# Row thresholds moved from VectorE to ScalarE, products with V of two units in one burst, and a new order of the whole program

## Chip, cores and metric

One NeuronCore of a Trainium2 chip runs the program. The metric is the device time of one execution in microseconds (us). TensorE, VectorE, ScalarE, GpSimd and SyncE appear in rows as PE, DVE, ACT, POOL and SP; PEld is TensorE's weight load.

## What is computed

Attention over 4 batches, 8 heads, 576 tokens and a head size of 64, then two feed-forward parts on 2304 tokens of 512 numbers:

```python
scores = scale * np.matmul(q, k.transpose(0, 1, 3, 2))
thresh = np.max(scores, axis=-1, keepdims=True) - tau
scores = np.where(scores >= thresh, scores, -1000000000.0)
attn = np.exp(scores - np.max(scores, axis=-1, keepdims=True))
attn = attn / (np.sum(attn, axis=-1, keepdims=True) + 1e-09)
x = np.matmul(attn, v)             # -> 2304 x 512
h = x @ w_in;  x = (h - np.tanh(h)) @ w_out
...                                # 8 experts: each token goes through the one with the largest logit
out[mask] = gate_w[mask, None] * eom[mask, e, None] * (np.maximum(x[mask] @ w1[e], 0.0) @ w2[e])
```

Of each row only the scores within `tau` of the row's maximum count.

## The kernel before

**Attention.** There are 32 units: a batch, a half of its tokens (256 or 320 queries) and a pair of heads, in this order, so a batch has four units of the first half and then four of the second. `attention(ui, ...)` (L1051) records one unit. For each tile of 128 queries and each head TensorE makes the scores `sp` in PSUM (L1085, in the first eight units L1096). VectorE scales them into `em` and keeps each row's minimum of the negated scores in `mx` (L1106, called **scan** below). ScalarE makes the exponentials `e` (L1109). The **threshold** is one addition for the tile: `tb = mx + tau`, 2 numbers per partition for both heads, or 1 for a third tile that both heads share (L1118, with the choice of engine in L1113). The **gate** (L1122, VectorE) keeps the exponentials whose score passes `tb` and sums each row into `rs`. TensorE turns the gated tile (`pt`, L1138), ScalarE moves it to SBUF (`eth`; the rest `elh`), and TensorE multiplies it by V (`pv`, L1193): ten matmuls per unit that write 64 columns of the array, issued as a burst of six and one of four (`BURST = (3, 2)`), between which other work may stand. The reciprocal sums are spread by ScalarE (`rb`, L1171), turned (L1208), and VectorE multiplies the result by them (`xf`, L1212).

**Feed-forward.** As soon as units have filled a chunk of 256 tokens, steps of the first feed-forward part on that chunk (`step`, L731: matmuls L743 and L777, ScalarE L756 to L762, VectorE L764 and L766, GpSimd L556) stand between the attention's instructions. VectorE also unpacks this part's weights (`conv`, L685 to L694). After the attention come the rest of this part, the routing and the eight experts.

**What sets the order.** Every instruction is recorded with an engine, a duration for the planner and the tiles that it reads and writes. `Sched.order` then plays the program through and writes each engine's instructions in the order of their start, by a table of numbers (`URGENCY`), one for each instruction. So one number moves rows on every engine, and an instruction whose planner duration changes can move too. Each engine then works through its list in order. Tiles come from rings: `em` has 5 buffers, `e` 3, `eth` and `elh` 2, `rb` 3 (`EMN, EN, ETN, RBN`).

`round_to` and `rest` (L551 to L575) are helpers, so their lines L554, L556, L558, L568 and L574 stand for many operations.

Of the kernel before, what the change touches and what calls it, by code (L numbers as in the profile page):

```python
# [17 lines left out]
ALU = mybir.AluOpType  # L18
# [34 lines left out]
EMN, EN, ETN, RBN = 5, 3, 2, 3  # L53
# [28 lines left out]
    'c-rk)_e0I^`+n_p_Bm}WqbRdfA{k{gsFV_gG^vo35s{EmR%GN|WF{+ARyJj&ge0<8Ml!NWzW4L$^Iv>De#m*9bDrlO*L_{rb24W{Y~J<E^zPq+'  # L82
    '8H0`2J<ACSua*BeJtTN*M&IV|;fvEYmpGpG+ZFq6U4%dD7VBweWWrVdSa2~~mzrN`=UzQII^M2R1@Y-vX*fNp$#=(@@Mz}2y{huJ9Q|~uO>c9%'
    '+hxvAjz>4G^j=Ch&F);+ZMk9bTccMaVssXDy}#@IwLJ<y{nC)w;;JI)I1_xLPM6@C#doi4J>zFEYv<kdm1Z%WUfeWpmSheH(chdEW%)L&xWG5L'
    'aBpidJ=hKp?5s`;vY7w-N8ql9GqsBk4VYP^iCJ*<q21U%^Hy{Y-sC*wlB?dgMTx$KEi0}rk5rUnQ++mmKC>g%XJ@V%u@Ad^ys)#@%hSY?5aN-w'
    'jeb?e?ebgB>b<=riQWDVi5jqaoaq*qSy`d8H@q3@UezsJ?`n#txm874QOTQ~kE&MvB+K|ihEIFZ-v>V!QR<r~_kLUU?PS&CXKY!6{p?Z83H>2g'
    'k{g$q&j~s8ZnFC7@$z!((}^pO+YO)9G{LtZB;mo8HBYb1xKbN<xZf&y{$t0`;x<1s8|-#jxsThH<)4^ZrFQ1{O+%Y&`UeL%>37K1RCqk^IIo9E'
    't$){hkC*3|o=8+MIWmvr$%-|1J688Muz2d>KHVnxSc0la?*#q9Y&G8Me=_n|Xv(&=Khl&FhXfuNGoa-*6Gd!OccunMyKPF}-0%7eZ~K--p$D`r'
    '^Uep<$sYM$IOTunkZp6!@w6WN*B!Q(p3m0G5kl(y3YHGv;PiN5*zCT+JL>`h2iIM#KAVy^dETIP)w1PP>w^vqsb8(Hs`^=+f5Fu8?(YRQWo6p8'
    '7w-7oafa2>ng12M%CG2TX07_F7&zVB>g8S4%NTXRCc`P6PE4Ek^H={9(@VaXnyzT*dM)9)bI$TbQ;Q1&_f*vSzbYf=pQt}PARuAJ0ea#~yY2HW'  # L90
    '>bFNEoHH-o>bJ6M>dWIUznW@3F3`O0Ww}N6GiSh%Wt;XFYHDw#H+FdO+V4ul=BSmf7UA};y<8gl1s?X^RI<56NBT)`>`U4GCSg|Mp~M1>*N!c!'
    'Qhr-#B7QbRGU=Ah!T96}zm<L2micdOHa}hbcjKZt_yzB#_kj^n|7D-{p3$@WSK@1ZxP_C?rDZucmF4@*^?wQ3^^z<n*Xp<<YU8L2t%GA7PsBz|'
    '5?bbr^M4YXPfyZhGX7Bmlhz#es<4Rea<P8$%T33WdJ$TadtHcJdAt)LX&p#k@6h*RpBFltHk^BL^=IYrVe5=PY&p2{o3mA$$?Ec*POtkjSvl*a'
    'W%*kDygaOW*j&HRC#%0huFm9@Ira^id4_SJKQBG1&)UBtu6065v1k0eN<}GlPw&Iw+@KQ&?Gq+mDY5r)oSk{LxB30lZ)W#1KN}rs95B;0bN{Kt'
    '$a^*T6+5djaqDA;Z}qqBJ@(?K84{&y{?@;}cXX)kuerN&a7sl#yMEy=kN1sEH=#C}tJ12r{I1QDUwcs+_hC-ctI=N+WI<vEnefeU&4Iz@9f!sa'
    'H>lZPHTY~!?=f1tH(%-BXTQI9Ug#9eWw1}s>5}w`yL_lFySnQ;ja@I_8>f4D+>~6#YguU};oS7qyy1Gt>|I~yZTX_QfBdgW?7RG`!vzsJlIV@t'
    '6pqiOX20=CTH)|JJyJM#QimP&%J`jk*j3)=m&KBGj`D%V6;q#ES%kh`KY-2r9YUC7evOPSEl*i9`}MStqVM@(nmJPCyf;Rj_S=o0yR?K%j*F`M'
    'IxV|`JH0N&YMIHc;NIEOepGwZM{1g0oiID?Joa*NO2gt$=a=O+U-98)`kWirp)~2>lIq6SF278pJa=d|&)iYj^iXB_@JX53{<-JQ9D3mHvi7Sy'
    'BBGAnFtNPV0;_aiVEAWC(*5uUi!TRb5&Dr1cNa$<zio5u=ir32j5}O)NLs?hOBL5|A7919+#BYwxxuz}%2%(M7s(L6)pLm>_9-W$B<Br!j`Fmw'
    'jIWqFewdYUd{+Zqw+$&z9~aDxjtP0$)NS)n?+LD!U5`$jo~n2^ewanupWLrri_bb@1|xRHt+#P<XnEJ-zw6O<%Yg74Jn4d*I=%5yUH{fFQ;W&c'  # L100
    '2Tp0rCN+3#KRbmbOpBGS`2KZl%bV<?h%>J)xAjkTe(rhOHTO{C+ht?@?=6yOy-d8x`(D3TC%u+&=I!8k?2{qswQARyyE)H;YC7o6IM!o(o_~k)'
    '4T}aWt}{7x*nz4x%o}F$uwQvEj})!ifTPvPOKrZSRSel{QTX@Je-j<98oQ?QM~fc?Et5P>GkFkvrOdHlZ)9cPPpoO-=?D4S)22Pf!j?q0#4g&~'
    'W>oh~-+W=pOQw{+P@jM44gKW^{?n&t<yF6%t{w&MvchPKk})5iA76NSt*v#U=Z9|RzHLp4W@p@SN>~%_YBK9VSpUMG+1fS+KG7ke54QUK{Ai=!'
    'TQYIvj-8~jxr@%2%zEp0BUD)yRw;M1b`PwXw8U=e@Ead%!a4=3C%PtYI9NX?>fWv~xdz@Hbz=OU5BPhhHe=xO8#A%OPKELFEt3}978-{XUF$t)'
    'f`i_@5%2#9UKTSlV#@2rJXSOBiYpEs$ru>&Y*GFaohKQi=7-mHmX{Zwu`-Rkt<`W;+kEOvF6+F3laDd?d3lEa5XJLg%7NRZ<Dd0BvO03b0sfLg'
    'dw-1U^~}SLy|U$pZ)qo$E?D&U!mrrJC7<sM`~8RQaWc!eV!KZF%e|aD{Th00O_(ufR@Sb-E9-xCX)KIn-3}QYCz}@cSyET~rsDXmzJ+_}Po6(U'
    'o=9WsB3-8)dDlVGL+|JDEWIm=iP7FmlyQ?bb(oi-DV)|Kf1a}@{J{R-YR};Bdp0-@j>w35>a(Rt=VLYN+O{{L(koeibGL{|FUF23u>Z=PnmHi%'
    'VEOvf&%5cEb+u7CXBI3T@M={4?9YXnw9$f*+XvnF6CYdq%=&cO<cN|#^IBX6n*KN5eY4g3)`siX{9NpIdd;Zu&G>Bl8n5>6EWP_~cS*-TZ6jn2'
# [347 lines left out]
def tile_main(ctx, tc, qa, qb, q2, kT, k3, vv, tau, w_in, w_out, gates, w1, w1b, w2, out, dbg=None):  # L456
# [594 lines left out]
    def attention(ui, k0, qs):  # L1051
# [132 lines left out]
        xf = buf("ep", "xf", 2, [P, 320])  # L1184
        dl += TAU
        pv = buf("ps_v", "pv", 1, [P, 4, P])
        pvf = lambda: pv.t.rearrange("p a b -> p (a b)")[:, 0:n]

        def pairs_(kts):
            for kt in kts:  # L1190
# [787 lines left out]
```

## Time and profile before

| | |
|---|---|
| time, median of 3 | 970.16 us (969.92 to 971.55) |
| profiled execution | 971.04 us, its span 969.2 us |
| TensorE busy | 940.4 us (97%) |
| VectorE busy | 727.5 us (75%) |
| ScalarE busy | 551.1 us (57%) |
| GpSimd busy | 346.0 us (36%) |
| granted clock of TensorE, mean | 0.998 |

Shares over the whole span mix stages with different limits, so the stretches of the span have to be read apart. A matmul is shown until its end in the pipeline, so a busy TensorE can hide short stalls; the spacing of starts tells more.

### The profile page before, as it was taken

The numbers are of one execution on the slowest core, as the hardware profiler recorded it, in microseconds if no ns is written. First come the engines' busy times: TensorE is split into PE (matmuls) and PEld (weight loads), VectorE is DVE, ScalarE is ACT, GpSimd is POOL, SyncE is SP. The second block draws the span as 40 slices with busy tenths as digits, with TensorE's granted clock in tenths as the row PEclk, the third lists the DMA queues.
The fourth block names the chain that finished last, engine by engine and source line by source line (L and its number), as shares of the span: only waits on it lengthen the run. The fifth ranks groups of instructions, "written<-read, shape, count | busy, mean of one in ns | idle before, by whom it ended". The sixth has DMA issues, their size and how long they took to land.

```text
span 969.2 us, 18499 instructions
## 1 busy us (share of the span) xinstructions
PE 940.4 (97%) x6636; PEld 806.5 (83%) x6636; DVE 727.5 (75%) x1812; ACT 551.1 (57%) x1142; POOL 346.0 (36%) x434
## 2 busy tenths in 40 slices
PE   8899889999999999999999999999999999999996
PEld 4556667888888888888899888888888899999996
DVE  7999999898789877857268668888676777646630
ACT  5888777777778767757445444344343434435421
POOL 1368548884667754434210101011012302213101
PEclk9999999999999999999999999999999999999999
DMA  9264645565664662451595366476854876655600
GB/s 268 102 204 150 195 139 183 170 206 169 198 215 160 193 244 86 132 182 45 180 364 175 118 189 158 130 169 137 266 177 144 271 229 229 193 169 165 214 14 32
DMA packets 71604, 168.70 MB, mean 174 GB/s; under 512 B 32382, under 2 KB 33022, under 8 KB 65616
## 3 DMA queue, kind: packets, MB, share of 16 engines
q1 hardware_dynamic: 67872, 157.41, 51.3%
q0 software_dynamic: 3200, 9.77, 2.9%
q8 instruction: 54, 0.88, 0.4%
q14 instruction: 46, 0.38, 0.1%
q10 hardware_dynamic: 432, 0.26, 0.1%
HBM read 125.99 MB, written 35.45 MB: 167 GB/s over the span
## 4 chain that ended last, share of the span: by engine, by line
PE 81%; DVE 14%; issue 2%; ACT 1%; DMA 1%; POOL 0%; POOLq 0%; DVEq 0%; ACTq 0%
PE x L777 20%; PE ph L743 20%; PE ph L1750 9%; PE py L1637 8%; PE sp L1085 5%; PE pv L1193 5%; DVE em L1122 5%; PE pt L1138 4%; DVE em L1106 3%; PE py L1783 2%; DVE ct L691 1%; PE pt L1682 1%; PE ph L1388 1%; DVE ct L694 1%; DVE tb L1118 1%
## 5 line engine op out<-in xcount | busy, mean ns | idle before, releaser
L743 PE MATMUL ph<-xh,wi 128*128 128x256 f32 x1152 | 178.1, 286 | 1.2 <-DVE u L766 1.1
L777 PE MATMUL x<-wo,gh 128*128 128x512 f32 x576 | 167.7, 404 | 0.0
L743 PEld LDWEIGHTS ph<-xh,wi 128*128 128x128 f32 x1152 | 156.3, 188 | 10.4 <-DVE u L766 3.1
L1122 DVE SCALAR_TENSOR_TENSOR em<-em,tb,e 128x576 f32<-128x576 f32 x144 | 142.4, 1003 | 8.0 <-ACT e L1109 5.0
L1109 ACT ACTIVATE e<-em,mx 128x576 f32<-128x576 f32 x144 | 110.8, 774 | 46.1 <-DVE em L1106 43.3
L1106 DVE TENSOR_SCALAR_CACHE_REDUCE em<-sp 128x576 f32<-128x576 f32 x144 | 107.6, 749 | 36.9 <-PE sp L1085 31.0
L556 POOL TENSOR_SCALAR gh<-u 128x512 fp32r<-128x512 f32 x52 | 38.4, 739 | 220.2 <-DVE u L766 168.5
L777 PEld LDWEIGHTS x<-wo,gh 128*128 128x128 f32 x576 | 99.0, 189 | 16.4 <-issue 1.3
L756 ACT ACTIVATE u<-ph 128x512 f32<-128x512 f32 x72 | 43.0, 598 | 94.2 <-PE ph L743 89.9
L764 DVE SCALAR_TENSOR_TENSOR w<-w,u 128x512 f32<-128x512 f32 x72 | 53.9, 748 | 53.6 <-ACT w L760 53.3
L743 PE MATMUL ph<-xl,wi 128*128 128x256 f32 x576 | 93.5, 284 | 0.0
L1138 PE MATMUL pt<-ident,em 128*128 128x128 f32 x576 | 84.3, 276 | 7.6 <-DVE em L1122 5.2
L554 ACT ACTIVATE eth<-pt 128x512 f32<-128x512 f32 (+1 forms) x160 | 84.6, 548 | 12.5 <-PE pt L1138 11.7
L777 PE MATMUL x<-wo,gl 128*128 128x512 f32 x288 | 90.6, 401 | 0.0
L1138 PEld LDWEIGHTS pt<-ident,em 128*128 128x128 f32 x576 | 65.6, 141 | 22.9 <-ACT eth L554 6.5
L743 PEld LDWEIGHTS ph<-xl,wi 128*128 128x128 f32 x576 | 79.6, 189 | 1.0
L1085 PE MATMUL sp<-kst,qh 128*128 128x288 f32 (+2 forms) x252 | 73.7, 311 | 2.9 <-DVE em L1106 2.8
L1193 PE MATMUL pv<-eth,vt 128*64 128x256 f32 (+1 forms) x512 | 71.6, 414 | 0.9 <-ACT elh L554 0.9
L1619 POOL DMA_INDIRECT out_dram<-o,ids x23 | 24.4, 1059 | 130.9 <-ACT o L1615 127.6
L1755 ACT ACTIVATE hh<-ph 128x320 fp32r<-128x320 f32 (+2 forms) x56 | 22.7, 420 | 83.2 <-PE ph L1750 82.9
L574 DVE TENSOR_TENSOR w<-wraw,w 128x512 fp32r<-128x512 f32 x98 | 65.5, 688 | 5.7 <-ACT w L554 4.3
L1085 PE MATMUL sp<-kst,ql 128*128 128x288 f32 (+2 forms) x252 | 68.0, 293 | 0.0
(380 smaller groups left out, 2003.7 us busy)
## 6 DMA issues: line engine op xcount, KB each, us to landing
wraw<-in_w_dram SPq DMA_DIRECT2D x60, 512.0 KB, 4.5
wi<-wsv SPq DMA_DIRECT2D x17, 1024.0 KB, 5.8
wo<-wsv SPq DMA_DIRECT2D x17, 1024.0 KB, 6.2
craw<-in_w_in_dram SPq DMA_DIRECT2D x14, 512.0 KB, 5.1
craw<-in_w_out_dram SPq DMA_DIRECT2D x14, 512.0 KB, 3.8
kr<-in_kT_dram SPq DMA_DIRECT2D x24, 288.0 KB, 4.6
wsv<-wi SPq DMA_DIRECT2D x6, 1024.0 KB, 4.6
wsv<-wo SPq DMA_DIRECT2D x6, 1024.0 KB, 5.9
```

What stands on the lines that cost most here:

```text
L554: return sc.add("ACT", act(n, psum), due, lambda: nc.scalar.activation(dst(), src(), AF.Copy), r, w)
L574: return sc.add(eng, dve(n, psum) + 5 if eng == "DVE" else pool_tt(n), due, lambda: e.tensor_tensor(out=dst(), in0=src(), in1=hi().bitcast ...
L743: nc.tensor.matmul(ph.t[:, j, :], wi.t[:, w_, cc * CH + j * P:cc * CH + (j + 1) * P], x_.t[:, cc, :], start=(n == 0 and cc == 0), stop=(n ...
L777: nc.tensor.matmul(x2b[c, half][t].t, g_.t[:, j, t * P:(t + 1) * P], wo.t[:, w_, j * DM:(j + 1) * DM], start=(first and n == 0 and j == 0) ...
L1085: nc.tensor.matmul(sp.t[:, kb_, o:o + w], q_.t[:, q0:q0 + P], kb.t[:, hh, c0:c0 + w], start=(i == 0), stop=(i == len(todo) - 1),)
L1106: sc.add("DVE", 665, d, lambda ev=ev, sp=sp, mx=mx: nc.vector.tensor_scalar(out=ev().rearrange("p (a b) -> p a b", a=2), in0=sp.t[:, :, 0: ...
L1109: sc.add("ACT", 667, d + 800, lambda e=e, ev=ev, mx=mx: nc.scalar.activation(e.t, ev(), AF.Exp, bias=mx(), scale=-1.0), [(em, h), (m2, h)] ...
L1122: sc.add("DVE", 729, d + TAU, lambda ev=ev, tb=tb, e=e, col=col: nc.vector.scalar_tensor_tensor(out=ev(), in0=ev(), scalar=tb(), in1=e.t, ...
L1138: nc.tensor.matmul(pt.t[:, kt, :], em.t[:, c0:c0 + P], ident, is_transpose=True, start=(kt == 0), stop=(kt == 3))
L1193: nc.tensor.matmul(pvf()[h * D:(h + 1) * D], vb_.t[:, k, :], eth[h].t[:, kt, 0:n] if kt < 4 else elh.t[:, 0:n], start=(kt == 0), stop=(kt ...
L1637: nc.tensor.matmul(py[k].t[:, 0:cap], wx()[:, k * P:(k + 1) * P], x_.t[:, 0:cap], start=(f == 0 and n == 0), stop=(f == 7 and n == 2))
L1750: nc.tensor.matmul(ph.t[:, 0:cap], wx()[:, cc * P:(cc + 1) * P], x_.t[:, cc, 0:cap], start=(n == 0 and cc == 0), stop=(n == 2 and cc == 3))
```

## The change

- The 80 thresholds go to ScalarE (`"thr"`). The operation for that engine was there already (L1115).
- In the third and fourth batch (`PAIRED = 2`), two units of the first half share one burst: 20 matmuls, no other work between, both results in one PSUM tile. Their `eth` and `elh` are held until then. All else keeps the bursts of six and four.
- `e` has 2 buffers instead of 3, `rb` 5 instead of 3.
- The planner's durations of VectorE operations are other numbers, and `URGENCY` is another table.

```diff
-EMN, EN, ETN, RBN = 5, 3, 2, 3
+EMN, EN, ETN, RBN = 5, 2, 2, 5
+PAIRED = 2
...
-    "x_h": "AP", "x_l": "P", "w_h": "AD", "w_l": "D", "w_l0": "D", "f_h": "A", "thr": "D", "eps": "D", "r_2": "DA",
+    "x_h": "AP", "x_l": "P", "w_h": "AD", "w_l": "D", "w_l0": "D", "f_h": "A", "thr": "A", "eps": "D", "r_2": "DA",
...
-    'c-rk)_e0I^`+n_p_Bm}WqbRdfA{k{gsFV_gG^vo35s{EmR%GN|WF{+ARyJj&ge0<8Ml!NWzW4L$^Iv>De#m*9bDrlO*L_{rb24W{Y~J<E^zPq+'
...
-                sc.add("DVE", 335, d, lambda t=t: nc.vector.tensor_scalar(
+                sc.add("DVE", 343, d, lambda t=t: nc.vector.tensor_scalar(
...
-                sc.add("DVE", 665, d, lambda ev=ev, sp=sp, mx=mx: nc.vector.tensor_scalar(
+                sc.add("DVE", 678, d, lambda ev=ev, sp=sp, mx=mx: nc.vector.tensor_scalar(
...
-                sc.add("DVE", 75, d + 801, lambda m2=m2, t2=t2, nt=nt: nc.vector.tensor_scalar(
+                sc.add("DVE", 133, d + 801, lambda m2=m2, t2=t2, nt=nt: nc.vector.tensor_scalar(
...
-                sc.add("DVE", 729, d + TAU, lambda ev=ev, tb=tb, e=e, col=col: nc.vector.scalar_tensor_tensor(
+                sc.add("DVE", 745, d + TAU, lambda ev=ev, tb=tb, e=e, col=col: nc.vector.scalar_tensor_tensor(
...
+        waiting.append((ui, dl + TAU, eth, elh, rbs))
+        if half or b < PAIRED or hp % 2:
+            products(waiting)
+            del waiting[:]
+        return dl + 5 * TAU
...
+    def products(todo):
...
+            k0_ = 0
+            for g in BURST if len(todo) == 1 else ():
+                sc.add("PE", (538 if half else 432) * g, dl, lambda k0_=k0_, g=g, pairs_=pairs_: pairs_(range(k0_, k0_ + g)),
+                       [vb_] + [elh] * (k0_ + g == 5) + eth, [(pv, i)], mode=1)
+                k0_ += g
+            runs.append((pairs_, [vb_, elh] + eth))
+            if len(todo) > 1 and i:
+                sc.add("PE", 432 * 10, dl, lambda: [f(range(5)) for f, _ in runs],
+                       [x for _, r in runs for x in r], [(pv, 0), (pv, 1)], mode=1)
```

The rest of `products` is the code of L1184 to L1226, for each of its one or two units. Its lines after the change: scan L1123, exponential L1126, threshold L1132, gate L1139, product L1223.

Three places show what the table moves. In the names a number tells buffers apart, and `em_310` before is `em_309` after.

VectorE where the first unit ends and the second begins, before:

```order
L1160 TENSOR_SCALAR rs_276<-rs_276 128x4
L685 TENSOR_SCALAR ct_337<-ct_337 128x512
L1118 TENSOR_SCALAR tb_354<-mx_311,tau_t_65 128x2
L1106 TENSOR_SCALAR em_356,mx_357<-sp_326 128x576
L688 TENSOR_SCALAR ct_337<-ct_337 128x512
L1162 RECIPROCAL rs_276<-rs_276 128x4
L1122 SCALAR_TENSOR_TENSOR em_310,rs_366<-em_310,tb_354,e_329 128x576
```

Here the threshold `tb_354` takes a place on VectorE ahead of the gate of its tile, `em_310`.

VectorE at that place, after the change:

```order
L1139 SCALAR_TENSOR_TENSOR em_277,rs_291<-em_277,tb_293,e_312 128x576
L705 TENSOR_SCALAR ct_335<-ct_335 128x512
L1177 TENSOR_SCALAR rs_291<-rs_291 128x4
L1123 TENSOR_SCALAR em_337,mx_338<-sp_342 128x576
L708 SCALAR_TENSOR_TENSOR ct_335<-craw_240,ct_335 128x512
L1179 RECIPROCAL rs_291<-rs_291 128x4
L1139 SCALAR_TENSOR_TENSOR em_309,rs_371<-em_309,tb_340,e_345 128x576
```

No threshold is left on VectorE, here or later.

ScalarE at that place, after the change:

```order
L1132 ACTIVATE tb_340<-mx_310,tau_t_65 128x2
L1126 ACTIVATE e_345<-em_309,mx_310 128x576
L571 ACTIVATE eth0_322<-pt_330 128x4x128
L1126 ACTIVATE e_353<-em_309,mx_310 128x576
L571 ACTIVATE eth1_327<-pt_355 128x4x128
L571 ACTIVATE elh_368<-pv_320 128x256
L1132 ACTIVATE tb_376<-mx_338,tau_t_65 128x2
L1188 ACTIVATE rb_378<-rs_291 128x128
```

The thresholds `tb_340` and `tb_376` now stand among ScalarE's exponentials and moves. Of the first 24 thresholds for two heads, 5 stand ahead of both exponentials of their tile, 15 between them and 4 behind both.

TensorE where the first two units of the third batch are multiplied by V, after the change (`vt_2283` and `vt_2490` are the two units' V):

```order
L1223 MATMUL pv_3356<-eth1_2935,vt_2283 64x256
L1223 MATMUL pv_3356<-elh_3308,vt_2283 64x256 x2
L1223 MATMUL pv_3356<-eth0_3225,vt_2490 64x256
L1223 MATMUL pv_3356<-eth1_3214,vt_2490 64x256
L1223 MATMUL pv_3356<-eth0_3225,vt_2490 64x256
L1223 MATMUL pv_3356<-eth1_3214,vt_2490 64x256
L1223 MATMUL pv_3356<-eth0_3225,vt_2490 64x256
L1223 MATMUL pv_3356<-eth1_3214,vt_2490 64x256
L1223 MATMUL pv_3356<-eth0_3225,vt_2490 64x256
L1223 MATMUL pv_3356<-eth1_3214,vt_2490 64x256
L1223 MATMUL pv_3356<-elh_3330,vt_2490 64x256 x2
L1102 MATMUL sp_3397<-kst_2839,qh_3130 128x288
```

Before, 19 rows of scores, turns and feed-forward work stood between these two units' products. Over the program the runs of adjacent products go from 41 to 36.

## Rows read from the trace of the kernel before

**Rows 1.** The page's first line.

```profile
span 969.2 us, 18499 instructions
```

**Rows 2.** Stretches: length, busy us (xinstructions) of PE, PEld, DVE, ACT, POOL; PEclk, DMA share, GB/s.

```profile
0.00:150.00 150.00, 131.35 (x890) 85.64 (x891) 141.35 (x366) 116.96 (x236) 78.75 (x108) 1.00 0.55 172
150.00:175.00 25.00, 24.41 (x166) 19.84 (x166) 23.76 (x46) 17.57 (x37) 20.33 (x25) 1.00 0.61 203
175.00:460.00 285.00, 284.02 (x2041) 241.36 (x2039) 229.67 (x517) 207.14 (x429) 166.16 (x217) 1.00 0.51 167
460.00:950.00 490.00, 488.93 (x3475) 449.62 (x3474) 331.30 (x882) 205.61 (x438) 76.89 (x82) 1.00 0.58 183
950.00:969.20 19.20, 11.70 (x71) 10.08 (x69) 1.42 (x4) 3.78 (x7) 3.84 (x4) 0.91 0.12 39
```

**Rows 3.** Waits of TensorE from 0 to 150 us: us in total, times, longest us.

```profile
PE pt L1138 <- DVE em L1122: 5.2, 9, 1.0
PE sp L1096 <- DVE em L1106: 4.0, 8, 1.2
PE sp L1085 <- DVE em L1106: 2.6, 5, 0.8
```

**Rows 4.** Waits of VectorE from 0 to 150 us.

```profile
DVE em L1106 <- PE sp L1096: 4.8, 2, 4.2
DVE ct L685 <- ACT ct L681: 1.0, 1, 1.0
```

**Rows 5.** VectorE's groups from 0 to 150 us: busy us, mean ns of one, idle us before them.

```profile
L1122 DVE SCALAR_TENSOR_TENSOR em<-em,tb,e 128x576 f32<-128x576 f32 x57 | 56.3, 994 | 0.9
L1106 DVE TENSOR_SCALAR_CACHE_REDUCE em<-sp 128x576 f32<-128x576 f32 x58 | 43.1, 747 | 5.0 <-PE sp L1096 4.8 <-PE sp L1085 0.2
...
L1118 DVE TENSOR_SCALAR tb<-mx,tau_t 128x2 f32<-128x2 f32 x26 | 9.0, 348 | 0.2
...
L1118 DVE TENSOR_SCALAR tb<-mx,tau_t 128x1 f32<-128x1 f32 x5 | 1.0, 197 | 0.0
```

**Rows 6.** VectorE in order of time: start us, us; three of its thresholds, each with its follower.

```profile
8.10 0.23 DVE L1118 TENSOR_SCALAR tb<-mx,tau_t 128x2 f32<-128x2 f32 x1
8.44 0.82 DVE L1122 SCALAR_TENSOR_TENSOR em<-em,tb,e 128x576 f32<-128x576 f32 x1
...
105.04 0.22 DVE L1118 TENSOR_SCALAR tb<-mx,tau_t 128x2 f32<-128x2 f32 x1
105.17 0.41 DVE L688 TENSOR_SCALAR ct<-ct 128x512 uint32<-128x512 uint32 x1
...
120.23 0.91 DVE L1118 TENSOR_SCALAR tb<-mx,tau_t 128x2 f32<-128x2 f32 x1
121.25 1.39 DVE L1122 SCALAR_TENSOR_TENSOR em<-em,tb,e 128x576 f32<-128x576 f32 x1
```

**Rows 7.** GpSimd in order of time, around the third of these thresholds.

```profile
119.80 2.22 POOL L568 TENSOR_TENSOR ql<-qr,qh 128x352 fp32r<-128x352 f32 x2 [3.88 <-ACT qh L554]
```

**Rows 8.** ScalarE's exponentials from 0 to 150 us, columns as in rows 5.

```profile
L1109 ACT ACTIVATE e<-em,mx 128x576 f32<-128x576 f32 x58 | 44.5, 774 | 20.8 <-DVE em L1106 19.1 <-DVE rs L1160 1.2
```

**Rows 9.** ScalarE's operation on 2 numbers per partition, whole span, columns as in rows 5.

```profile
L906 ACT ACTIVATE eo<-og 128x2 f32<-128x2 f32 x9 | 1.8, 200 | 4.8 <-DVE og L905 4.8
```

**Rows 10.** TensorE in order of time around one burst of products with V.

```profile
230.56 0.63 PE L777 MATMUL x<-wo,gl 128*128 128x512 f32 x2
231.03 0.29 PE L1085 MATMUL sp<-kst,qh 128*128 128x288 f32 x1
...
231.56 0.62 PE L777 MATMUL x<-wo,gl 128*128 128x512 f32 x2
232.11 2.38 PE L1193 MATMUL pv<-eth,vt 128*64 128x320 f32 x16
234.31 0.71 PE L1193 MATMUL pv<-elh,vt 128*64 128x320 f32 x4
234.95 1.09 PE L1138 MATMUL pt<-ident,em 128*128 128x128 f32 x8
```

More of the change, by code (lines that the diff above doesn't have):

```diff
@@ L87 @@
[L87 to L96, printed above, removed]
@@ L187 @@
[L187 to L191 removed]
+    'c-rlk=T{WjxA&{6t2$P9Rdvoe=Wd{(Ns@C^i3%v9f+E2HA}FG$m~+k<bIxJRIbs;Im~{-JV^(A?>-i7vy7yV@x9;-uqFz;<I%n_w-TQl>ZaG^W'
@@ L1183, in attention @@
             round_to("p_h2", D, dl + 500, lambda: elh.t[D:P, 256:320], lambda: plf()[D:P, 320:384], slots, [elh], True)
-        xf = buf("ep", "xf", 2, [P, 320])
-        dl += TAU
-        pv = buf("ps_v", "pv", 1, [P, 4, P])
-        pvf = lambda: pv.t.rearrange("p a b -> p (a b)")[:, 0:n]
-        def pairs_(kts):
-            for kt in kts:
-                for h in range(2):
-                    k = 2 * kt + h
-                    nc.tensor.matmul(
-                        pvf()[h * D:(h + 1) * D], vb_.t[:, k, :],
-                        eth[h].t[:, kt, 0:n] if kt < 4 else elh.t[:, 0:n], start=(kt == 0), stop=(kt == 4))
@@ L1227, in attention, with pairs_ @@
-        return dl + 2 * TAU
+        waiting.append((ui, dl + TAU, eth, elh, rbs))
[3 more added lines that the diff above has]
+        return dl + 5 * TAU
+    waiting = []
+    def products(todo):
+        dl = todo[-1][1]
+        pv = buf("ps_v", "pv", 1, [P, 4, P])
+        xfs, runs = [], []
+        for i, (ui, _, eth, elh, rbs) in enumerate(todo):
+            b, half, hp = units[ui]
+            n = 320 if half else 256
+            vb_ = vts[b, hp]
+            pvf = lambda i=i, n=n: pv.t.rearrange("p a b -> p (a b)")[:, 256 * i:256 * i + n]
+            def pairs_(kts, pvf=pvf, vb_=vb_, eth=eth, elh=elh, n=n):
+                for kt in kts:
+                    for h in range(2):
+                        nc.tensor.matmul(
+                            pvf()[h * D:(h + 1) * D], vb_.t[:, 2 * kt + h, :],
+                            eth[h].t[:, kt, 0:n] if kt < 4 else elh.t[:, 0:n], start=(kt == 0), stop=(kt == 4))
+            k0_ = 0
[7 more added lines that the diff above has]
+                       [x for _, r in runs for x in r], [(pv, 0), (pv, 1)], mode=1)
+        for i, (ui, _, eth, elh, rbs) in enumerate(todo):
+            b, half, hp = units[ui]
+            n = 320 if half else 256
+            pvf = lambda i=i, n=n: pv.t.rearrange("p a b -> p (a b)")[:, 256 * i:256 * i + n]
+            xf = buf("ep", "xf", 2, [P, 320])
+            xfs.append(xf)
+            round_to("bot", n, dl + 1200, lambda xf=xf, n=n: xf.t[:, 0:n], pvf, [(pv, i)], [xf], True)
+        for (ui, _, eth, elh, rbs), xf in zip(todo, xfs):
+            b, half, hp = units[ui]
+            n = 320 if half else 256
+            d = dl + 2 * TAU
+            rp = buf("ps_v", "pv", 1, [P, 4, P])
+            rpf = lambda rp=rp: rp.t.rearrange("p a b -> p (a b)")
+            for qt, rb in enumerate(rbs):
+                if qt < 2:
+                    sc.add("PE", 109, d, lambda qt=qt, rb=rb, rp=rp: nc.tensor.transpose(rp.t[:, qt, :], rb.t, ident), [rb], [(rp, qt)])
+                else:
+                    sc.add("PE", 120, d, lambda qt=qt, rb=rb, rp=rp: nc.tensor.matmul(
+                        rp.t[:, qt, 0:D], rb.t, sel, start=True, stop=True), [rb], [(rp, qt)])
+            eng = pick("xm")
+            e_ = nc.vector if eng == "DVE" else nc.gpsimd
+            sc.add(eng, dve(n, True) + 5 if eng == "DVE" else pool_tt(n) + 60, d + 400, lambda rpf=rpf, xf=xf, n=n, e_=e_: e_.tensor_tensor(
+                out=xf.t[:, 0:n], in0=xf.t[:, 0:n], in1=rpf()[:, 0:n], op=ALU.mult), [rp], [xf])
+            t0 = b * S + half * 256
+            o = 0
+            while o < n:
+                c, r = divmod(t0 + o, CH)
+                m = min(CH - r, n - o)
+                xh, xl = chunk(c)
+                hi = lambda xh=xh, r=r, m=m, hp=hp: xh.t[:, hp, r:r + m]
+                src = lambda o=o, m=m, xf=xf: xf.t[:, o:o + m]
+                reg = (hp, r)
+                round_to("x_h", m, d + 1500, hi, src, [xf], [(xh, reg)])
+                rest("x_l", m, d + 1500, lambda xl=xl, r=r, m=m, hp=hp: xl.t[:, hp, r:r + m], src, hi,
+                     [xf, (xh, reg)], [(xl, reg)])
+                o += m
```

260 lines of the change are left out of this document (128 added, 132 removed), and 2 rows, old and new, of the table ENGINES.

## The prediction

> **What bounds the kernel now.** I read the stretches of the span first, then the waits of TensorE and VectorE in the stretch where TensorE idles, then the groups of that stretch, and at last single rows. The span is 969.2 us [rows 1]. From 175 to 950 us TensorE is busy in 284.02 of 285 and 488.93 of 490 us [rows 2]: there it is the bound, and 2.1 us of idle time are all that another engine could give back. The last 19.2 us hold 7.5 us of idle time, but that is the end of the program. The first 150 us are another stage: TensorE is busy for 131.35 us, so it idles for 18.65, while VectorE is busy for 141.35 of 150 and ScalarE for 116.96 [rows 2]. What TensorE waits for there is VectorE: 5.2 us for gates before a turn, and 4.0 and 2.6 us for scans that have to free a score tile [rows 3]. VectorE hardly waits: 4.8 us for the very first scores and 1.0 us for ScalarE [rows 4]. So in the first 150 us VectorE sets the pace, until enough feed-forward work is there for TensorE. A microsecond taken from VectorE before about 150 us brings the rest of TensorE's list forward by up to a microsecond; one taken after it meets a TensorE that is full anyway.
>
> **The change, part by part.** Counted in the orders, up to the last gate of the twelfth unit VectorE has the same instructions before and after, but for 28 thresholds that are gone; up to that unit's last product TensorE has the same matmuls, in another order. So in the stage that counts, the new table only shuffles, and the move of the thresholds is the net change. (This and the other counts of order are no times.)
>
> *Thresholds off VectorE.* By 150 us there are 26 for two heads and 5 for one [rows 5]. What one costs varies. At 105.04 us the next instruction starts 0.13 us later. At 8.10 us its own gate follows, and that starts 0.34 us after it, since it needs the result. At 120.23 us it lasts 0.91 us, and GpSimd runs a two-input operation from 119.80 on for 2.22 us [rows 6, 7]; the gate behind it then takes 1.39 us against a mean of 0.99 [rows 5, 6], so such a wait would mostly fall on the next instruction if the threshold were gone. Lower bound: 31 x 0.13 = 4.0 us. Upper bound: the groups' whole busy time, 9.0 + 1.0 = 10.0 us [rows 5]. I take 0.13 for two thirds of them and 0.34 for one third, without the waits that look like GpSimd's: 21 x 0.13 + 10 x 0.34 = 6.1 us, nearer to the lower bound since the waits are not the threshold's own.
>
> *Thresholds on ScalarE.* No row shows the operation there. The nearest is its exponential on 2 numbers per partition, 0.200 us [rows 9]; the far end is the large exponential's 0.774 us [rows 8]. The operation is as small as the near one, so 31 x 0.20 = 6.2 us, bounds 6.2 and 24.0. ScalarE idles for 33 us of the 150 [rows 2], 19.1 of them because a scan is not done [rows 8], so it has room for the likely sum. What counts is what waits for it: behind a threshold on ScalarE stand an exponential or a move of a turned tile, and behind those a gate or the next turn. Gates now wait for 0.9 us in total over 57 of them [rows 5], so exponentials come early. A threshold that lands between the two exponentials of its tile delays the second by 0.2 us, which that slack hides as a rule; if the cover were gone for all 31, it would cost 6.2 us. I book 1.0 us (0 to 6.2).
>
> *Two `e` buffers instead of three.* An exponential now waits for the gate two before it. Two buffers turn over in about one exponential and one gate, 0.774 + 0.994 = 1.8 us for two gates, while the stage makes 57 in 150 us, one in 2.6 us [rows 5, 8]. Nothing is booked; where gates stand close together it can cost some tenths, which is in the 1.0 us above.
>
> *Bursts.* A pair of matmuls takes 231.03 - 230.56 = 0.47 us when scores follow and 232.11 - 231.56 = 0.55 us when a burst follows, so entering costs 0.08 us. The sixteen matmul records of the burst take 2.20 us, 0.138 each, so four would take 0.55; the last four take 0.64 until the turns start, so leaving costs 0.09 [rows 10]. That is 0.17 us for a run, and 41 runs become 36: 0.9 us, all of it on a full TensorE. Bounds: 0 if something else already stands in those gaps, and 0.9.
>
> *Holding `eth` for two units.* Until the shared burst no later unit of the batch can move a turned tile to SBUF. The cover is feed-forward work, of which TensorE has enough after 175 us [rows 2]; nothing is booked, and without the cover it is a rival below.
>
> *The other 49 thresholds, five `rb` buffers, the planner's durations, the shuffle after 175 us.* The thresholds leave a VectorE that is busy for 229.67 of 285 us beside a full TensorE [rows 2]: nothing, at most the stretch's 1.0 us of idle time. The durations change no operation. The shuffle can make new waits as well as end old ones; 2.1 us of idle time bound what it can give, and I book 0.
>
> **Sum**, against the profiled execution's 971.04 us: - 6.1 + 1.0 - 0.9 = - 6.0 us, 965.0. The median of the runs is 970.16, 0.9 lower, so the same steps give **964.2 us**.
>
> **Rivals.**
>
> *A. ScalarE's queue takes the place of VectorE's threshold (slower).* Place: each gate of the first 150 us. A threshold stands in ScalarE's list behind exponentials and moves, and the gate, which had its threshold from its own engine, waits for it. In favour: ScalarE is the second-busiest engine there, 117 us before the change [rows 2], and 4 of the first 24 stand behind both exponentials of their tile, 15 between them. Against: gates wait for only 0.9 us now [rows 5], and ScalarE itself waits for scans [rows 8]. Price: its own 0.20 us [rows 9] plus the 0.11 us between a threshold's end and its gate's start (8.33 to 8.44) [rows 6], 0.31 if it just misses, up to 0.20 + 0.774 = 0.97 if a whole exponential is ahead. It decides from (6.1 + 0.9) / 31 = 0.23 us of new waiting for each threshold. At 0.31 the time is 970.16 + 31 x 0.31 - 7.0 = 972.8 us; at 0.97 it is 993.
>
> This is what the Trainium skill would have one expect: ScalarE: Activation LUTs, Rules for kernel authors, tells to use VectorE and not ScalarE for an addition. Its section What ACT_TABLE_LOAD costs gives about 280 ns + 0.833 ns per element for an operation whose bias is read from a tile, as here: an estimate from that page is 0.28 us, 31 x 0.28 = 8.7 us on ScalarE. By the rule the forecast's gain would turn into rival A's loss. The trace of before bears it out only in part: in this stage VectorE is the fuller engine by 24 us, and the rule does not weigh that.
>
> *B. The relief is hidden.* VectorE's freed time is eaten by the waits beside GpSimd, which only move to the next instruction, and by waits of two engines that now alternate. In favour: the third threshold of rows 6. Against: even there 0.13 us per threshold is issue time of its own. Only the bursts are left: 970.16 - 0.9 = 969.3 us.
>
> *C. The held tiles stall.* In each of the four shared bursts the next units' turns wait for their buffers, and TensorE runs dry for part of a burst; a burst of 20 records is 2.8 us [rows 10], two units are less than twice that. With 1 us lost at each, 964.2 + 4 = 968.2 us; with a whole burst of 2.8 at each, 975.
>
> **How the numbers follow.** A measurement of this kernel tells a difference of about 0.2%, 1.9 us, from none, so faster is below 968.2 and slower above 972.1. Forecast 0.67, its own range 960 to 968: the high end has the lower bound of the relief with 2.0 us more of waiting (970.16 - 4.0 + 2.9 - 0.9 = 968.2), the low end the upper bound (970.16 - 10.0 - 0.9 = 959.3, with some waiting 960). A 0.13, B 0.13, C 0.07. Faster takes the forecast and half of C, 0.70; same takes B, the rest of C and a little of A, 0.17; slower most of A, 0.13. The range is 960 to 971.5: it holds the forecast, B and C, and leaves out A.
>
> **What would show it.** In the profile after: no threshold on VectorE, 80 on ScalarE at some 0.2 us each; TensorE idle for 12 to 14 us in the first 150 instead of 18.65; gates that still wait for little; VectorE's gates of the twelfth unit some 5 us earlier; from 175 us on no new waits on TensorE. The prediction is wrong if gates begin to wait for ScalarE (A), if idle time in the first 150 us is unchanged (B), or if the gain of that stage is given back later (C or the shuffle).

## The result and the profile after

The changed kernel takes **959.97 us** (median of 4 runs, 958.63 to 961.27), the kernel before beside it 970.27 us. The ratio is 0.9891, with a 95% interval of 0.9874 to 0.9909. So it is faster by 10.3 us, where 6.0 were forecast, and the median lies just below the lower end of the range. A later series of the same kernel gave 959.6 us and a ratio of 0.9887 (0.9872 to 0.9902).

The profiled execution took 958.63 us. Its stretches, with the columns of [rows 2]:

```profile
0.00:150.00 150.00, 137.53 (x949) 92.42 (x950) 140.78 (x350) 127.89 (x280) 88.85 (x116) 1.00 0.55 180
150.00:175.00 25.00, 25.00 (x170) 19.63 (x168) 20.72 (x39) 19.49 (x44) 19.74 (x23) 1.00 0.64 194
175.00:460.00 285.00, 284.73 (x2051) 244.82 (x2048) 211.37 (x464) 211.40 (x470) 166.84 (x214) 1.00 0.50 169
460.00:950.00 490.00, 488.76 (x3474) 451.13 (x3472) 330.44 (x882) 203.56 (x430) 80.01 (x82) 1.00 0.59 181
```

In the first 150 us TensorE idles for 12.47 us instead of 18.65 and does 949 matmuls instead of 890. VectorE is as full as before, 140.78 us, and ScalarE is fuller, 127.89. The page says of the whole span:

```profile
PE 936.3 (98%) x6636; PEld 808.0 (84%) x6636; DVE 703.3 (74%) x1732; ACT 563.0 (59%) x1222; POOL 356.4 (37%) x434
```

TensorE's waits from 0 to 150 us, for [rows 3]: for gates 2.6 us instead of 5.2, for scans 4.7 instead of 6.6.

```profile
PE pt L1155 <- DVE em L1139: 2.6, 5, 1.1
PE sp L1113 <- DVE em L1123: 2.6, 6, 1.1
PE sp L1102 <- DVE em L1123: 2.1, 4, 0.9
```

VectorE's waits in the same stretch, for [rows 4]; gates wait for thresholds on ScalarE, but little:

```profile
DVE em L1123 <- PE sp L1113: 4.6, 2, 4.5
...
DVE em L1139 <- ACT tb L1132: 0.6, 2, 0.4
```

VectorE's groups in that stretch, for [rows 5]. There are two gates and three scans more than before, and the mean gate is 31 ns shorter:

```profile
L1139 DVE SCALAR_TENSOR_TENSOR em<-em,tb,e 128x576 f32<-128x576 f32 x59 | 56.2, 963 | 1.0 <-ACT tb L1132 0.6
L1123 DVE TENSOR_SCALAR_CACHE_REDUCE em<-sp 128x576 f32<-128x576 f32 x61 | 45.5, 750 | 5.8 <-PE sp L1113 4.6 <-PE sp L1102 0.8 <-PE pv L1194 0.3
```

The threshold on ScalarE, over the whole span: 291 ns, where the nearest row [rows 9] had 200.

```profile
L1132 ACT ACTIVATE tb<-mx,tau_t 128x2 f32<-128x2 f32 (+1 forms) x80 | 23.1, 291 | 10.2 <-DVE em L1123 9.7
```

Two more readings are used below. The first is when the twelfth unit's last gate starts. Before, VectorE in order of time:

```profile
133.68 1.49 DVE L1122 SCALAR_TENSOR_TENSOR em<-em,tb,e 128x576 f32<-128x576 f32 x1
```

and after, 8.4 us earlier:

```profile
125.30 0.82 DVE L1139 SCALAR_TENSOR_TENSOR em<-em,tb,e 128x576 f32<-128x576 f32 x1
```

The second is TensorE's **lost time**, since a busy TensorE hides short stalls. I worked it out from the starts of all 6636 matmuls: for each, the distance to the next start, less what that form takes undisturbed (117 ns for 128x256, 131 for 128x288, 231 for 128x512, 108 for a turn, 105 and 131.5 for the products with V). Added up by stretch, in us; the last four columns are experiments told below. Two traces of the changed kernel differ by at most 0.4 us in a stretch:

```
us          before   after   all on VectorE   first 28   later 52   old order, on ScalarE
0-150        37.7    30.4        35.1           34.5       31.3            37.3
150-300      10.2     7.3         9.7            7.9        8.3            10.3
300-475       8.9     7.6         8.0            7.8        8.4             9.6
475-end      13.6    13.8        14.0           13.9       14.1            13.4
sum          70.5    59.1        66.8           64.1       62.1            70.6
```

So 7.3 us were gained in the first 150 us, and 4.2 between 150 and 475 us, where the prediction expected 0.9. By its records TensorE is as good as full from 175 to 460 us in both kernels (284.02 and 284.73 of 285 us), so most of that gain lies in stalls that the records do not show as idle.

### The profile page after: what moved, and what is told of

It reads as the page before. It is cut to its first block, busy times and chain, and to the rows that moved or that the text cites. A ratio compares the mean times of both kernels' runs of the same rounds, so it can differ in the third digit from the quotient of the medians.

```text
span 956.8 us, 18477 instructions
## 1 busy us (share of the span) xinstructions
PE 936.3 (98%) x6636; PEld 808.0 (84%) x6636; DVE 703.3 (74%) x1732; ACT 563.0 (59%) x1222; POOL 356.4 (37%) x434
## 4 chain that ended last, share of the span: by engine, by line
PE 81%; DVE 9%; issue 6%; ACT 3%; POOL 1%; POOLq 0%; ACTq 0%; DVEq 0%
PE x L794 21%; PE ph L760 20%; PE ph L1794 7%; PE py L1681 7%; PE sp L1102 6%; PE pv L1223 6%; PE pt L1155 4%; DVE em L1139 3%; DVE em L1123 2%; PE py L1827 2%; PE ph L1432 1%; PE pt L1726 1%; ACT e L1126 1%; ACT eth L571 1%; PE pt L1695 1%
## 5 line engine op out<-in xcount | busy, mean ns | idle before, releaser
L1139 DVE SCALAR_TENSOR_TENSOR em<-em,tb,e 128x576 f32<-128x576 f32 x144 | 140.2, 990 | 16.9 <-ACT tb L1132 13.0
L1123 DVE TENSOR_SCALAR_CACHE_REDUCE em<-sp 128x576 f32<-128x576 f32 x144 | 108.0, 751 | 40.5 <-PE sp L1102 34.9
L1126 ACT ACTIVATE e<-em,mx 128x576 f32<-128x576 f32 x144 | 111.0, 774 | 24.7 <-DVE em L1123 17.0
L1223 PE MATMUL pv<-eth,vt 128*64 128x256 f32 (+1 forms) x512 | 70.8, 413 | 1.0 <-ACT elh L571 0.8
L794 PEld LDWEIGHTS x<-wo,gl 128*128 128x128 f32 x288 | 51.5, 189 | 9.7
```

What stands on the lines that cost most here:

```text
L794: nc.tensor.matmul(x2b[c, half][t].t, g_.t[:, j, t * P:(t + 1) * P], wo.t[:, w_, j * DM:(j + 1) * DM], start=(first and n == 0 and j == 0) ...
L1123: sc.add("DVE", 678, d, lambda ev=ev, sp=sp, mx=mx: nc.vector.tensor_scalar(out=ev().rearrange("p (a b) -> p a b", a=2), in0=sp.t[:, :, 0: ...
L1126: sc.add("ACT", 667, d + 800, lambda e=e, ev=ev, mx=mx: nc.scalar.activation(e.t, ev(), AF.Exp, bias=mx(), scale=-1.0), [(em, h), (m2, h)] ...
L1139: sc.add("DVE", 745, d + TAU, lambda ev=ev, tb=tb, e=e, col=col: nc.vector.scalar_tensor_tensor(out=ev(), in0=ev(), scalar=tb(), in1=e.t, ...
L1223: nc.tensor.matmul(pvf()[h * D:(h + 1) * D], vb_.t[:, 2 * kt + h, :], eth[h].t[:, kt, 0:n] if kt < 4 else elh.t[:, 0:n], start=(kt == 0), ...
```

## The experiments

**The move undone in the new order.** The order was left as it is, and the threshold's operation alone put on VectorE at the place that it has in the order, for all 80, for the 28 of the first twelve units, or for the other 52 (`ui` is the unit's number):

```diff
-                sc.add("ACT", 187, d + 801, lambda m2=m2, t2=t2, nt=nt: nc.scalar.activation(
+                vec = True                      # or ui < 12, or ui >= 12
+                sc.add("ACT", 187, d + 801, lambda m2=m2, t2=t2, nt=nt, vec=vec: nc.vector.tensor_scalar(
+                    out=t2.t[:, 0:nt], in0=m2.t[:, 0:nt], scalar1=tau_t, scalar2=None, op0=ALU.add) if vec else nc.scalar.activation(
```

The yardstick:

> The changed kernel once more, as the yardstick of this series: about 960 us, 10.3 below the kernel before (ratio 0.989). No theory is told apart here.

All 80:

> The changed kernel with its own order, but all 80 thresholds run on VectorE at the places that they have in the order. Theory T (in the first 12 units every threshold took a whole slot of some 0.3 us of VectorE, and TensorE got 7.3 us of that back; the later thresholds cost nothing): 960 + 7 = 967 us, TensorE's idle time in the first 150 us back from 12.5 to 17 or more. Rival L (the 49 later thresholds cost as well, through stalls too short to be shown as idle time, and the 4 us gained from 150 to 475 us are theirs): 960 + 7 + 4 = 971. Rival O (the new order brought the gain, the thresholds little): 960 to 963.

The first 28:

> The changed kernel with its own order, with the 28 thresholds of the first 12 units on VectorE and the other 52 on ScalarE. Theory T: 967 us, as with all of them. Rival L: 967 too. Rival O: 960 to 962.

The later 52:

> The changed kernel with its own order, with the 28 thresholds of the first 12 units on ScalarE and the other 52 on VectorE. Theory T: 960 us, no difference from the changed kernel. Rival L: 963 to 965. Rival O: 960.

Measured: 959.6 us for the yardstick, **966.3** with all on VectorE (ratio 0.9953, 0.9940 to 0.9967), **963.8** with the first 28 (0.9935, 0.9922 to 0.9949), **961.75** with the later 52 (0.9909, 0.9894 to 0.9924), beside 970.8 for the kernel before. So in this order the move is worth 6.7 us: 4.2 for the first 28 and 2.2 for the later 52, whose interval against the yardstick only just overlaps, but whose lost time rises in each of the first three stretches. Theory T and rival L each had one half: the early ones bring less than T said, and the later ones are not free. Rival O falls. What is left, 970.8 - 966.3 = 4.5 us, belongs to the new order with its bursts and rings, and to where the rings put the tiles.

With the first 28 back on VectorE, its groups from 0 to 150 us have them again; those for two heads have a mean record of 376 ns:

```profile
L1141 DVE SCALAR_TENSOR_TENSOR em<-em,tb,e 128x576 f32<-128x576 f32 x58 | 55.8, 968 | 0.5
...
L1133 DVE TENSOR_SCALAR tb<-mx,tau_t 128x2 f32<-128x2 f32 x24 | 8.9, 376 | 0.0
```

Records overlap, so I also added up, to the twelfth unit's last gate, the time from each VectorE start to the next. The thresholds take 8.1 us of that, 0.29 each. Yet the gate starts at 129.6 us, only 4.3 later than in the changed kernel. The other 8.1 - 4.3 = 3.8 us the changed kernel spends behind VectorE's other instructions, whose slots (from one start to the next) are longer there. Little of it is waiting: VectorE's idle time up to that gate rises by 0.9 us. The slots of the weights' unpacking (`ct`) grow by 1.6 us, those of the sums `rs` by 1.6 and those of `w` by 0.8, while those of the gates shrink by 0.7. The long records of `ct` and `rs` run beside an operation of GpSimd. One of them, on VectorE and on GpSimd in the changed kernel; with the thresholds back the same instruction takes 0.20 us:

```profile
84.73 0.77 DVE L1177 TENSOR_SCALAR rs<-rs 128x5 f32<-128x5 f32 x1
...
84.47 1.00 POOL L585 TENSOR_TENSOR kst<-kr,kst 64x288 fp32r<-64x288 f32 x1
```

So other instructions take over about half of what VectorE saves. One trace fixes such a time to about 1.5 us: the run with all 80 on VectorE has the same list up to this gate and starts it at 131.07 us, since one scan there waits 1.5 us for its scores.

The later 52, in the stretch from 150 to 475 us, with the columns of [rows 2]:

```profile
150.00:475.00 325.00, 324.05 (x2302) 276.25 (x2301) 252.76 (x566) 227.66 (x473) 190.09 (x244) 1.00 0.53 176
```

and the changed kernel in the same stretch:

```profile
150.00:475.00 325.00, 324.73 (x2318) 278.18 (x2317) 237.07 (x518) 235.01 (x521) 191.48 (x245) 1.00 0.53 179
```

Idle time differs by 0.7 us, but 16 matmuls fewer fit into the same 325 us. That is how a full engine still loses.

**The new order with all thresholds on VectorE, against the kernel before.** The same run as above tells what the order does alone. TensorE's waits from 0 to 150 us with all 80 on VectorE:

```profile
PE sp L1113 <- DVE em L1123: 4.4, 8, 1.1
PE pt L1157 <- DVE em L1141: 3.7, 5, 1.5
PE sp L1102 <- DVE em L1123: 2.1, 4, 0.7
```

The waits for gates fall from 5.2 us [rows 3] to 3.7, those for scans stay. The twelfth unit's last gate, with the same VectorE instructions up to there, starts 2.6 us before that of the kernel before, and 4.1 us before it in the run with the first 28 back. The two rows:

```profile
131.07 0.81 DVE L1141 SCALAR_TENSOR_TENSOR em<-em,tb,e 128x576 f32<-128x576 f32 x1
...
129.59 0.81 DVE L1141 SCALAR_TENSOR_TENSOR em<-em,tb,e 128x576 f32<-128x576 f32 x1
```

With all 80 on VectorE, lost time falls by 2.6 us to 150 us and by 1.4 from there to 475. One thing besides the order shows in that later stretch. In the kernel before, ScalarE and GpSimd wait there for the sums' turn to free one of the three `rb` buffers; with five, no such wait is left in the changed kernel, nor with all 80 on VectorE. What those waits cost was not tried.

```profile
ACT rb L1171 <- PE pv L1208: 2.5, 3, 1.1
...
POOL rb L1168 <- PE pv L1210: 1.8, 1, 1.8
POOL rb L1168 <- PE pv L1208: 1.0, 1, 1.0
```

**The move made in the old order.** The kernel before, in its own order; the threshold's operation alone runs on ScalarE (the edit, shortened):

```diff
-                sc.add("DVE", 75, d + 801, lambda m2=m2, t2=t2, nt=nt: nc.vector.tensor_scalar(
-                    out=t2.t[:, 0:nt], in0=m2.t[:, 0:nt], scalar1=tau_t, scalar2=None, op0=ALU.add), [m2, tau_m], [t2])
+                sc.add("DVE", 75, d + 801, lambda m2=m2, t2=t2, nt=nt: nc.scalar.activation(
+                    t2.t[:, 0:nt], m2.t[:, 0:nt], AF.Identity, bias=tau_t), [m2, tau_m], [t2])
```

> The kernel before with its own order, but all 80 thresholds run on ScalarE, at the places that they had in the order on VectorE. Theory M (the move is worth what undoing it cost in the new order, 966.3 - 959.6 = 6.7 us, and the new order with its bursts and rings the other 4.5): 964 us, and TensorE's idle time in the first 150 us down from 18.7 to some 15. Rival W (in the old order the gate stands right behind its threshold, so it now waits for ScalarE, as rival A of the prediction has it): 968 to 975. Rival P (the move is worth the whole 11 us and the new order nothing): 960.

Measured: 970.0 us, ratio 0.9991 (0.9982 to 1.0000): next to nothing, and within rival W's numbers. VectorE's waits from 0 to 150 us show why:

```profile
DVE em L1124 <- ACT tb L1120: 6.5, 14, 1.0
```

VectorE's busy time falls from 141.35 to 135.58 us, and gates wait for thresholds for 6.5 us instead. Theory M, that the move has a worth of its own, falls with that.

**The same, with each threshold ahead of its tile's last exponential on ScalarE.** Nothing else is moved (the list of places is edited before it is written out):

```diff
+        order = early(self.ops, order)     # a threshold goes ahead of the exponential recorded just before it, if it stood behind
```

> As the run with all thresholds on ScalarE in the old order (970.0 us), but each threshold that stood behind its tile's last exponential on ScalarE now stands ahead of it; nothing else moves. Theory Q (the move brings nothing there because gates wait for thresholds that are late in ScalarE's list, 6.5 us in the first 150 us): those waits fall below 2 us and the time to 964 to 967. Rival S (each threshold ahead holds up the exponential and what is queued behind it, so the wait only changes its name): 969 to 972.

Measured: 968.3 us, ratio 0.9978 (0.9969 to 0.9986). The wait is halved:

```profile
DVE em L1141 <- ACT tb L1137: 3.3, 6, 1.1
```

and the twelfth unit's last gate comes at 130.67 us instead of 132.04. So three orders give a series: gates wait 6.5, 3.3 and 0.6 us for thresholds, and the move is worth 0.8, 2.1 and 6.7 us. The waits fell less than theory Q said, and the time with them; where on ScalarE a threshold stands is part of the answer, and the rest of the order is another.

**The switch alone, planned anew.** `"thr": "A"` in the kernel before, under its old table of numbers.

> The kernel before with its own table of numbers, the thresholds on ScalarE, and the order planned anew from that: the switch alone. Theory M: 962 to 966, since the planner can now place the thresholds on ScalarE. Rival F (a table fits one program only, so any change of the program loses what the table had tuned): 970 or more.

Measured: 999.9 us, ratio 1.030 (1.0284 to 1.0315). Rival F. The first stretch, with the columns of [rows 2]:

```profile
0.00:150.00 150.00, 130.82 (x848) 84.77 (x848) 127.24 (x312) 114.01 (x246) 75.58 (x105) 0.95 0.54 171
150.00:475.00 325.00, 315.14 (x2219) 264.36 (x2219) 243.35 (x529) 239.04 (x528) 185.93 (x236) 1.00 0.49 163
```

VectorE is down to 127 us of 150, TensorE does 848 matmuls instead of 890, and its granted clock is 0.95 there instead of 1.00. The same move in the old order cost nothing, so it is the order that loses the time here. A table tuned for one program can be a bad one for its neighbour, and a comparison under such a table tells little of the edit.

**Without shared bursts.** Two attempts. In the first, `PAIRED = 4` (no batch left that shares bursts), with the changed table carried over and planned anew. In the second, the changed kernel's order is written down, and the first unit's products (with all that follows from them) are taken out of the shared burst and put ahead of the second unit's turned rest.

> The changed kernel without shared bursts: each unit of the third and fourth batch multiplies with V by itself, in a burst of six and one of four, and the first unit's numbers in the table are shifted by the distance between the units. By the prediction's term (5 runs at 0.17 us) 0.9 us more: 960.5 us. Rival B (the bursts carry the rest of the 4.5 us): 963 or more, with the loss between 200 and 475 us. Rival C turned round (the held tiles cost): 959 or less.

> The changed kernel with its own order written down, but in the four shared bursts the first unit's ten products (and what follows from them) are taken out and put ahead of the second unit's turned rest, as an own burst. The prediction's term: 4 more runs at 0.17 us, 0.7 us more, 960.3 us. Rival B (the shared bursts carry more of the 4.5 us that the thresholds don't): 961.5 to 963. Rival C turned round: 958 to 959.

Measured: 970.05 us (0.9996, 0.9987 to 1.0005) and 980.35 us (1.0105, 1.0091 to 1.0120). Neither tells what the bursts are worth. In the first, lost time from 400 to 475 us, mostly behind the last place of a shared burst, is 7.8 us instead of 3.6, and after 475 us 18.6 instead of 13.8: the table does not fit, as above. In the second the first unit's chain of products, moves and sums stands without a gap, and lost time rises by some 20 us around the four places; that comes from my edit. The turned rests, the products and the sums of both units go through one ring of a single PSUM tile, so the order has to be rebuilt around a split burst, and no small edit separates it.

What can be read is the burst itself. TensorE in order of time, after: a shared burst of 40 matmuls.

```profile
238.61 1.95 PE L1223 MATMUL pv<-eth,vt 128*64 128x256 f32 x16
240.39 0.60 PE L1223 MATMUL pv<-elh,vt 128*64 128x256 f32 x4
240.82 1.90 PE L1223 MATMUL pv<-eth,vt 128*64 128x256 f32 x16
242.55 0.60 PE L1223 MATMUL pv<-elh,vt 128*64 128x256 f32 x4
243.08 0.40 PE L1102 MATMUL sp<-kst,qh 128*128 128x288 f32 x1
```

Before, a single one of the same width:

```profile
251.47 1.95 PE L1193 MATMUL pv<-eth,vt 128*64 128x256 f32 x16
253.24 0.60 PE L1193 MATMUL pv<-elh,vt 128*64 128x256 f32 x4
253.77 0.62 PE L743 MATMUL ph<-xh,wi 128*128 128x256 f32 x3
```

Two singles are 2 x 2.30 = 4.60 us, the shared one 4.47: 0.13 us, and 0.08 for entering [rows 10] is saved besides. For 5 runs that makes 1.0 us, near the 0.9 of the prediction.

**Three buffers for `e`.** Only the tile's number of buffers, `bufs=3`, in the changed kernel's own order.

> The changed kernel with its own order, but three buffers for e instead of two. By the prediction two buffers cost nothing: 959.6 us, within 1 us. If the exponentials wait for the gate two before them, up to 4 us less (ScalarE now idles 4.4 us for gates in the first 150 us): 956 to 958.

Measured: 958.8 us, ratio 0.9882 (0.9866 to 0.9897) against the yardstick's 0.9887. So two buffers cost nothing that a run of this kernel can tell.

**More operations on VectorE and on ScalarE.** For each of the first 28 thresholds a second addition, into a tile that nobody reads, on VectorE in one kernel and on ScalarE in the other; the real one stays on ScalarE.

```diff
+    td_t = const.tile([P, 2], F32, name="td_t")
...
+                    if more:
+                        nc.vector.tensor_scalar(      # or nc.scalar.activation, as the real one
+                            out=td_t[:, 0:nt], in0=m2.t[:, 0:nt], scalar1=tau_t, scalar2=None, op0=ALU.add)
```

> The changed kernel with its own order and an additional addition of the threshold's kind on VectorE for each of the first 28 thresholds, whose result nobody reads; the real ones stay on ScalarE. It prices VectorE's slot alone. From the undone move of the same 28 (4.2 us more): 963 to 964. If the slots are worth 0.30 us each and all of it reaches TensorE: 968. If the price was the gate's waiting for its threshold and not the slot: 960 to 961.

> The changed kernel with its own order and each of the first 28 thresholds twice on ScalarE, the second into a tile that nobody reads: 28 more operations of 0.29 us, 8.2 us of ScalarE. By the prediction's term (1.0 us for 31 thresholds, most of them hidden): 960 to 961. If ScalarE's queue is as tight as VectorE's: 964 or more.

Measured: 961.1 us (0.9905, 0.9892 to 0.9919) and 957.75 us (0.9873, 0.9858 to 0.9887). The second kernel does more and is no slower than the yardstick, and both lose less after 475 us (12.4 and 12.5 us) than the changed kernel (13.8), with the same instructions there. The new tile moves all tiles behind it in SBUF, so it was tried alone:

```diff
+    td_t = const.tile([P, 2], F32, name="td_t")
```

In the changed kernel:

> The changed kernel with its own order and one more tile of 8 bytes per partition among the constants, which nobody uses; all later tiles of that pool and the pools above it lie elsewhere. Theory A (where tiles lie in SBUF moves TensorE's spacing): 957.5 to 958.5 us, with stalls after 475 us some 1.3 us lower. Rival N (no effect, the kernels with doubled thresholds differ for another reason): 959.6.

With three `e` buffers:

> Three buffers for e and the 8-byte tile together. If both help and add up: 957 us; if the third buffer for e only moved tiles as well: 958 to 959.

In the kernel before:

> The kernel before with the 8-byte tile. Theory A: it changes too, by up to 2 us either way (968.5 to 972.5). Rival N: 970.5.

Measured: **957.05 us** in the changed kernel (0.9861, 0.9846 to 0.9876), 956.8 with three `e` buffers (0.9862, 0.9847 to 0.9877) and 969.0 in the kernel before (0.9984, 0.9975 to 0.9993). So 957.05 is the baseline for the two, which ran in the series before it: 28 additions more cost **4.0 us on VectorE**, and 0.7 us on ScalarE, which is not told from nothing (the ratios' intervals overlap). The first is close to the 4.2 us of the move undone, so it is VectorE's slot that costs, and not the gate's waiting for its threshold. The two kernels' groups from 0 to 150 us, VectorE's addition:

```profile
L1136 DVE TENSOR_SCALAR td_t<-mx,tau_t 128x2 f32<-128x2 f32 x24 | 9.0, 375 | 0.0
```

and ScalarE's:

```profile
L1136 ACT ACTIVATE td_t<-mx,tau_t 128x2 f32<-128x2 f32 x24 | 7.0, 291 | 0.0
```

The 24 for two heads take 7.0 us of ScalarE or 9.0 of VectorE, not far apart, but only VectorE's show in the time: one engine sets the pace and the other does not.

## Why the prediction was right and wrong

- **The bound.** Right. VectorE sets the pace in the first 150 us; 28 small additions more or less there move the end by 4 us.
- **Thresholds off VectorE, - 6.1 us, and on ScalarE, + 1.0 us.** Together - 5.1 for the early ones; the run that undoes them shows 4.2. That is near by luck, since two sizes inside were off and nearly cancelled. The slot was 0.29 us and not 0.20, because the long thresholds came free as a whole; but only about half of the freed time was left at the twelfth unit's last gate. The step "such a wait would mostly fall on the next instruction" was wrong of the gates (a mean of 968 ns with the early thresholds back, 963 without) and partly right of the unpacking and the sums, whose slots grew by 3.2 us. ScalarE's operation took 0.29 us and not 0.20, and its price of 1.0 us is not contradicted (0.7 measured, not told from nothing).
- **Two `e` buffers, nothing.** Right within the measurement.
- **Bursts, - 0.9 us.** Right in size by the spacing, 0.21 us for a run; not shown by a run of its own. **Held tiles, nothing, and rival C.** TensorE's waits after 150 us come to 1.4 us in all, none of them for `eth` or at a shared burst.
- **"The other 49 thresholds ... nothing, at most the stretch's 1.0 us of idle time."** Wrong: 2.2 us for 52. The step took idle time in TensorE's records for all that could be lost. From 150 to 475 us the kernel before had 1.6 us of recorded idle time, but 19.1 us of lost time.
- **"So in the stage that counts, the new table only shuffles", and "2.1 us of idle time bound what it can give, and I book 0".** Wrong, and **the step that failed**. The same VectorE instructions in the new order reach the twelfth unit's last gate 2.6 to 4.1 us earlier (by two traces), and the order with its bursts and rings is worth 4.5 us, of which the bursts explain about one. Counting equal instructions says nothing of how long they wait for each other. Hence the sign "VectorE's gates of the twelfth unit some 5 us earlier" came out at 8.4: 4.3 by the thresholds and 4.1 by the order. Since the low end of the range (959.3, then 960) was made from the thresholds' upper bound and the bursts alone, it had no room for this term. (At the high end the 2.9 should be 1.0 + 2.0 = 3.0, which changes nothing.)
- **The sum.** Booked 5.1 + 0.9 = 6.0 us; measured 4.2 + 2.2 + 4.5 = 10.9 from separate kernels, 10.3 and 11.2 in the two direct comparisons.
- **Rival A.** Not in this kernel, but real: in the old order the same move brings 6.5 us of gates waiting for ScalarE and no gain. My estimate from the Trainium skill's page ScalarE: Activation LUTs, section What ACT_TABLE_LOAD costs, 0.28 us, agrees with the measured 0.291. The same page of the Trainium skill, section Rules for kernel authors, would keep an addition on VectorE, and the runs say that this depends on which engine is full: 28 additions cost 4.0 us on VectorE. Another page of the Trainium skill that I had not weighed, Perfetto Trace Analysis, section Optimizing Scalar/DVE Operations, says that with VectorE saturated it may make sense to give ScalarE some work, and here that agrees with 4.2 us. **Rival B** was right in part: other instructions of VectorE, many of them beside GpSimd, took over about half of the freed time. But it left the thresholds no gain at all, and undoing their move costs 4.2 us.

What stays open is which part of the new order brings its 3.5 us beside the bursts. Places on ScalarE for other work and GpSimd's operations beside VectorE's were not tried apart, and neither was the rings' moving of tiles, told of below. By lost time 2.6 of the 4.5 us lie in the first 150 us, where no wait for `rb` shows. The 1.4 from there to 475 us are little more than the bursts' 1.0, so five `rb` buffers can have brought little. Against the moved tiles speaks that the tile added below changes lost time mainly after 475 us, where the new order gains nothing.

## What to carry to other kernels

Moving an operation off the engine that sets the pace is worth what the list of the receiving engine allows: the same 80 operations moved gave 0.8, 2.1 and 6.7 us in three orders. When an order is written anew, book a term for it, bounded by the stalls between starts, not by the idle time of an engine whose records overlap. And compare two versions only in orders that were each made for them, or in one order written down: planned anew under a table that was not made for it, the kernel before took 999.9 us.

## What was not expected of the hardware

A tile of 8 bytes per partition that nobody uses, among the constants, moved all later tiles in SBUF and made both kernels faster, by 1.3 us before (ratio 0.9984, 0.9975 to 0.9993) and by 2.6 after (957.05 against 959.6, where the two intervals just overlap). The stretch from 475 to 940 us of the kernel before, and then with the tile; its busy time is the same to 0.01 us, and 10 matmuls more fit in:

```profile
475.00:940.00 465.00, 463.93 (x3315) 428.37 (x3314) 326.92 (x874) 197.52 (x419) 71.80 (x75) 1.00 0.60 188
```

```profile
475.00:940.00 465.00, 463.93 (x3325) 428.90 (x3325) 327.07 (x874) 198.56 (x421) 72.04 (x76) 1.00 0.59 188
```

In the changed kernel the same stretch goes from 3328 matmuls to 3338. The mean distance of starts of the feed-forward part's 864 128x512 matmuls, without those over 260 ns, falls by about 1 ns in both: from 233.2 to 232.2 in the kernel before and from 233.3 to 232.3 in the changed one. Lost time falls by 1.5 and 1.4 us after 475 us; ahead of that it stays the same in the kernel before and rises by 0.7 in the changed one. With the tile in both, the two kernels are 969.0 - 957.05 = 11.9 us apart, without it 11.2, so the gain does not hang on this shift. Why the place in SBUF matters was not tried; that it does means that an edit which adds or resizes a tile can carry an error of one to three microseconds of this kernel's 960. The fastest kernels of this study are the changed one with that tile, alone (957.05 us) or with three `e` buffers (956.8 us), which are not told apart.
